# Cross-covariance attention with a mixture-of-depths step: the gate for held stores moved by one load, and the gate's vector spread by a matmul

## The chip, the cores and the metric

The kernel runs on one core of a Trainium2 chip. A core has five engines that run their own instruction streams: TensorE (PE; its weight loads are listed as PEld), VectorE (DVE), ScalarE (ACT), GpSimd (POOL) and SyncE (SP). Sixteen DMA engines move data between the memory (HBM) and the core's own memory (SBUF). The metric is the time of one execution on the device in microseconds (us), as the median of several runs. The profile is of one execution; its span, 264.0 us, is a little shorter than the time of that run, 265.82 us.

## What is computed

The reference, cut to what matters:

```python
# q, k, v: (4, 6208, 256) fp32; tau = 1; w_gate: (256,); w1: (256, 1024); w2: (1024, 256)
qn = q / (norm(q, axis=1) + 1e-6)              # norm of each channel over the 6208 rows
kn = k / (norm(k, axis=1) + 1e-6)
a  = softmax(kn.transpose(0, 2, 1) @ qn / tau) # 256 x 256 for each batch
x  = v @ a                                     # (4, 6208, 256)

scores = x @ w_gate                            # one number for each row
for b in range(4):
    top_idx = the 128 rows of batch b with the highest scores
    ye = relu(x[b, top_idx] @ w1) @ w2
    out[b, top_idx] = x[b, top_idx] + sigmoid(scores[b, top_idx])[:, None] * ye
# all other rows: out = x
```

For each batch all of q and k must be read before `a` is known, and all of v before the 128 rows can be chosen. q, k and v are 76 MB together, the output is 25 MB.

## The kernel before

The rows of a batch are cut into six chunks of 1024 rows (8 for each of the 128 partitions) and a rest of 64. q, k and v are read by GpSimd's queue, with a cast to bf16 on the way. The list of loads, `units`, has the order in which they are needed; a load is issued as soon as its pool has a free buffer (four pairs of q and k chunks, six v chunks).

```python
    QK_BUFS = 4
    V_BUFS = 6
    ...
    def emit_load(u):                       # q and k of a chunk, or v of a chunk
        ...
                    ins = nc.gpsimd.dma_start(out=t, in_=view(src, b, ci))
        ...
        load_inst[u] = ins

    pump(4)                                 # the first four units: four pairs of q and k
```

Next come the two weight matrices, on SyncE's queue, and constants. The vector `w_gate` is wanted in every partition, and the kernel before reads it 128 times:

```python
        for dst, src, inner in ((w1_sb, moe_w1, F), (w2_sb, moe_w2, D)):
            raw = st_pool.tile([P, RPP, C], F32, name="stage")...
            nc.sync.dma_start(out=raw, in_=src.rearrange("(k p) n -> p k n", p=P))
            nc.scalar.copy(dst, raw)
    ...
    ones_f = const.tile([P, P], F32)
    nc.vector.memset(ones_f, 1.0)
    ...
    wg_bcast = const.tile([P, C], F32)
    nc.sync.dma_start(out=wg_bcast, in_=moe_w_gate.partition_broadcast(P))

    wrow = const.tile([P, B, NCOL + 1], F32)       # and more small constants on VectorE
    ...
    pump()                                  # further loads, as buffers come free
```

The first pass over a batch multiplies chunks of q and k on TensorE. When the last row of a chunk has been used, its buffers are free:

```python
            for cc in range(2):
                nc.tensor.matmul(s_ps[:, cc, :], lhsT=ks[:, sl], rhs=qs, ...)
                nc.tensor.matmul(g_ps[:, cc, :], lhsT=qs[:, sl], rhs=qs[:, sl], ...)
                nc.tensor.matmul(g_ps[:, 2 + cc, :], lhsT=ks[:, sl], rhs=ks[:, sl], ...)
```

The softmax follows, whose last stage is the first reader of the vector:

```python
            nc.vector.tensor_tensor_reduce(out=awj, in0=a_sb[:, cc, :], in1=wg_bcast, ...,
                                           accum_out=aw[:, cc:cc + 1])
```

The second pass transposes v (`vt_ps`), forms the output rows (`o_ps`) and copies them to `stage`, 1 MB each, from which SyncE's queue stores them. The selection of the 128 rows is cut into small stages that are put between other work. The program's order is kept on every engine (`tc.manual_schedule()`): instructions run in the order in which the code emits them.

Some stores of the second and third batch are held back (`deferred`), so that they do not share the DMA engines with the loads that the end of the run waits for. The first of them waits for one of the last loads, and the others come after it on the same queue:

```python
    def flush_deferred(n=1000):

        while deferred and n > 0:
            st = emit_store(*deferred.pop(0))
            if not gate_done:
                gate_done.append(1)
                tc.add_manual_dep(
                    st.ins, load_inst[units[-3]].ins.name,
                    mybir.DependencyInfo(mybir.DependencyClass.Sync, mybir.DependencyReason.DATA),
                    reason="stores behind the last loads")
            n -= 1
```

The last units are the seven v loads of the last batch: `units[-1]` is the rest of 64 rows, `units[-2]` the sixth chunk, `units[-3]` the fifth, `units[-4]` the fourth.

Of the kernel before, what the change touches and what calls it, by code (L numbers as in the profile page):

```python
# [9 lines left out]
F32 = mybir.dt.float32  # L10
# [7 lines left out]
P = 128  # L18
# [8 lines left out]
def kernel(  # L27
# [12 lines left out]
    nc = tc.nc  # L40

    B, N, C = q.shape
# [23 lines left out]
    const = ctx.enter_context(tc.tile_pool(name="const", bufs=1))  # L66
# [15 lines left out]
    ps_m = ctx.enter_context(tc.tile_pool(name="ps_m", bufs=1, space=PS))  # L82
# [66 lines left out]
    units = []  # L149
# [6 lines left out]
    load_inst = {}  # L156
# [67 lines left out]
    ones_f = const.tile([P, P], F32)  # L224
# [15 lines left out]
    nc.gpsimd.iota(iota_col, pattern=[[0, 1]], base=0, channel_multiplier=1,  # L240
                   allow_small_or_imprecise_dtypes=True)
    wg_bcast = const.tile([P, C], F32)
    nc.sync.dma_start(out=wg_bcast, in_=moe_w_gate.partition_broadcast(P))


    wrow = const.tile([P, B, NCOL + 1], F32)
# [16 lines left out]
    rhs = const.tile([P, NCOL + 4], BF16)  # L263
# [270 lines left out]
    def emit_store(b, ci):  # L534
        st = stage_of.pop((b, ci))
        ins = nc.sync.dma_start(out=view(out, b, ci), in_=st if ci < NFULL else st[:REM, 0, :])
        stores.append((b, ins))
        for o, sca in scatters:
            if o != b:
                tc.declare_no_dep(ins.ins, sca.ins, reason="rows of different batches")  # L540
        return ins
# [215 lines left out]
# [4 lines that stand above are left out]
            if not gate_done:  # L761
                gate_done.append(1)
                tc.add_manual_dep(
                    st.ins, load_inst[units[-3]].ins.name,
                    mybir.DependencyInfo(mybir.DependencyClass.Sync, mybir.DependencyReason.DATA),
                    reason="stores behind the last loads")
            n -= 1
# [70 lines left out]
    keep_warm(8)  # L838
    advance(side)
    flush_deferred()  # L840
    while side2:
        advance(side2)
# [52 lines left out]
```

## Time and profile before

| what | value |
|---|---|
| time, median of 3 runs | 265.98 us (265.81 to 266.06) |
| span of the profiled execution | 264.0 us |
| PE busy | 201.2 us (76%) |
| DVE busy | 121.2 us (46%) |
| ACT busy | 81.5 us (31%) |
| POOL busy | 55.7 us (21%) |
| DMA, moved as counted at its writing side | 66.97 MB, mean 254 GB/s |
| HBM read and written | 79.04 MB and 25.95 MB |

The busy time is the union of an engine's instructions over the span. The page also cuts the span into 40 slices of 6.6 us and gives for each the busy share of every engine in tenths. A chain of waits is followed back from the last instruction: at each step it names what released it. Lines such as `L291` are lines of the kernel's source; `x24` is a count; in square brackets behind an instruction stands the idle time before it and what ended it. In tables by stretches the last three columns are TensorE's granted clock, the share of DMA engines that were busy, and GB/s.

### The profile page before, as it was taken

Reading aid. Unit: us, or ns where it says so; the run is one execution under the profiler, and the core shown is the slowest. Engines: PE = TensorE matmul, PEld = TensorE weight load, DVE = VectorE, ACT = ScalarE, POOL = GpSimd, SP = SyncE. Lnnn points to the kernel's source line nnn. Section 1 sums busy time; section 2 is a strip of 40 time slices with the busy share of each in tenths; the row PEclk is TensorE's granted clock in tenths of the full one; section 3 lists DMA queues with packets and bytes.
Section 4 is the critical chain, followed back from the end, with each engine's and each line's share of the span. In section 5 each row is a group of like instructions: output and inputs, shape, how many; then the busy total and the mean of one; then the engine's idle time right before and its main releaser. Section 6 shows DMA issues by size and latency. Waiting matters only on the chain.

```text
span 264.0 us, 6087 instructions
## 1 busy us (share of the span) xinstructions
PE 201.2 (76%) x2584; PEld 177.0 (67%) x2584; DVE 121.2 (46%) x464; ACT 81.5 (31%) x146; POOL 55.7 (21%) x104
## 2 busy tenths in 40 slices
PE   0194987899937677799986886899999899789700
PEld 0183876789926566589975775898999688578500
DVE  0200002614404366613436985674885827867400
ACT  3101100167720000117730100435102866795200
POOL 7113124121110023321300324320432003010110
PEclk9997699999998799799989999999999999999965
DMA  7999999999999999999999999999999999999950
GB/s 221 228 228 229 216 209 217 210 217 277 320 317 317 297 216 211 214 214 210 313 317 246 213 213 221 214 212 214 214 209 213 213 290 400 416 389 406 420 246 0
DMA packets 17642, 66.97 MB, mean 254 GB/s; under 512 B 2000, under 2 KB 4688, under 8 KB 14544
## 3 DMA queue, kind: packets, MB, share of 16 engines
q0 software_dynamic: 12384, 38.93, 73.8%
q1 hardware_dynamic: 5232, 27.66, 26.5%
q8 instruction: 20, 0.33, 0.4%
q14 instruction: 6, 0.05, 0.0%
HBM read 79.04 MB, written 25.95 MB: 398 GB/s over the span
## 4 chain that ended last, share of the span: by engine, by line
DMA 54%; PE 19%; issue 12%; DVE 8%; POOL 2%; ACT 1%; POOLq 1%; DVEq 0%; SPq 0%
DMA k_ch<-in_k_dram 22%; DMA q_ch<-in_q_dram 17%; DMA v_ch<-in_v_dram 12%; PE o_ps L477 5%; PE s_ps L291 4%; DMA out_dram<-stage 3%; PE g_ps L293 2%; PE vt_ps L403 2%; PE g_ps L295 2%; DVE cnt L588 1%; DVE cmp L584 1%; PE sc_ps L431 1%; DVE junk L310 1%; DVE stage L483 1%; PE g_ps L477 1%
## 5 line engine op out<-in xcount | busy, mean ns | idle before, releaser
L291 PE MATMUL s_ps<-q_ch,k_ch 128*128 128x256 bf16 x384 | 97.4, 293 | 30.1 <-DMA k_ch<-in_k_dram 29.5
L293 PE MATMUL g_ps<-q_ch 128*128 128x128 bf16 x384 | 89.0, 232 | 1.1 <-DVE nsq L310 1.0
L295 PE MATMUL g_ps<-k_ch 128*128 128x128 bf16 x384 | 88.9, 232 | 0.0
L291 PEld LDWEIGHTS <-k_ch 128*128 128x128 bf16 x384 | 40.3, 105 | 35.1 <-DMA k_ch<-in_k_dram 32.1
L295 PEld LDWEIGHTS <-k_ch 128*128 128x128 bf16 x384 | 40.2, 105 | 8.7 <-issue 1.6
L477 PE MATMUL o_ps<-a_sb,vt_sb 128*128 128x256 bf16 x298 | 43.9, 271 | 1.9 <-ACT vt_sb L410 1.3
L485 ACT COPY stage<-o_ps 128x512 f32<-128x512 f32 x68 | 38.3, 590 | 15.6 <-PE o_ps L477 15.6
L293 PEld LDWEIGHTS <-q_ch 128*128 128x128 bf16 x384 | 40.2, 105 | 1.2 <-issue 0.9
L412 DVE COPY vt_sb<-vt_ps 128x1024 bf16<-128x1024 bf16 (+1 forms) x33 | 20.8, 633 | 31.2 <-PE vt_ps L403 31.2
L477 PEld LDWEIGHTS <-vt_sb 128*128 128x128 bf16 (+1 forms) x376 | 29.4, 97 | 8.1 <-issue 4.4
L403 PE MATMUL vt_ps<-ident_b,v_ch 128*128 128x128 bf16 x336 | 24.6, 219 | 1.4 <-DMA v_ch<-in_v_dram 0.7
L431 PEld LDWEIGHTS <-vt_sb 128*128 128x128 bf16 (+1 forms) x376 | 23.8, 96 | 2.5 <-DVE sc L552 0.2
L174 POOL DMA_DIRECT2D q_ch<-in_q_dram x23 | 12.7, 553 | 59.9 <-PE g_ps L295 38.2
L403 PEld LDWEIGHTS <-v_ch 128*128 128x128 bf16 x384 | 22.2, 97 | 3.8 <-DMA v_ch<-in_v_dram 2.6
L306 ACT COPY s_sb<-s_ps 128x512 f32<-128x512 f32 x4 | 2.3, 586 | 71.3 <-PE s_ps L291 41.1
L431 PE MATMUL sc_ps<-aw_sb,vt_sb 128*128 128x2 bf16 (+1 forms) x376 | 24.2, 164 | 0.0
L310 DVE CUSTOM_DVE_ANT_0 junk<-g_ps,ident_f 128x128 f32<-128x128 f32 x16 | 4.6, 290 | 38.7 <-PE g_ps L295 38.3
L174 POOL DMA_DIRECT2D v_ch<-in_v_dram x24 | 12.8, 540 | 23.3 <-DMA k_ch<-in_k_dram 11.2
L174 POOL DMA_DIRECT2D k_ch<-in_k_dram x23 | 12.6, 546 | 21.8 <-PE o_ps L477 10.7
L588 DVE TENSOR_REDUCE cnt<-cmp 128x7 bf16<-128x343 bf16 x28 | 14.4, 513 | 1.0
L410 ACT COPY vt_sb<-vt_ps 128x1024 bf16<-128x1024 bf16 x11 | 10.6, 1011 | 12.8 <-PE vt_ps L403 12.7
L584 DVE SCALAR_TENSOR_TENSOR cmp<-u,delta,shares 128x343 bf16<-128x343 f32 x24 | 13.9, 578 | 0.9
(156 smaller groups left out, 213.0 us busy)
## 6 DMA issues: line engine op xcount, KB each, us to landing
out_dram<-stage SPq DMA_DIRECT2D x24, 1024.0 KB, 9.1
v_ch<-in_v_dram POOLq DMA_DIRECT2D x24, 512.0 KB, 14.8
q_ch<-in_q_dram POOLq DMA_DIRECT2D x23, 512.0 KB, 17.0
k_ch<-in_k_dram POOLq DMA_DIRECT2D x23, 512.0 KB, 17.4
stage<-in_moe_w_dram SPq DMA_DIRECT2D x2, 1024.0 KB, 14.6
q_ch<-in_q_dram POOLq DMA_DIRECT2D x2, 256.0 KB, 8.9
k_ch<-in_k_dram POOLq DMA_DIRECT2D x2, 256.0 KB, 9.7
out_dram<-stage_rem SPq DMA_DIRECT2D x4, 64.0 KB, 8.0
```

Of the source, the lines that this page charges most:

```text
L174: ins = nc.gpsimd.dma_start(out=t, in_=view(src, b, ci))
L291: nc.tensor.matmul(s_ps[:, cc, :], lhsT=ks[:, sl], rhs=qs, start=first and cc == 0, stop=last and cc == 1)
L293: nc.tensor.matmul(g_ps[:, cc, :], lhsT=qs[:, sl], rhs=qs[:, sl], start=first and cc == 0, stop=False)
L295: nc.tensor.matmul(g_ps[:, 2 + cc, :], lhsT=ks[:, sl], rhs=ks[:, sl], start=False, stop=last and cc == 1)
L403: nc.tensor.transpose(vt_ps[:, cc, j, :parts], in_=vt[:parts, s0 + j, cc * P:(cc + 1) * P], identity=ident_b[:parts, :parts])
L410: nc.scalar.copy(vt_sb[:, :, :n, :parts], vt_ps[:, :, :n, :parts])
L412: nc.vector.tensor_copy(vt_sb[:, :, :n, :parts], vt_ps[:, :, :n, :parts])
L431: nc.tensor.matmul(sc_ps[:parts, col, :], lhsT=vt_sb[:, cc, j, :parts], rhs=aw_sb[:, cc, :], start=cc == 0 and col in (0, NCOL - 1), stop= ...
L477: nc.tensor.matmul(o_ps[:parts, pj, :], lhsT=vt_sb[:, cc, j, :parts], rhs=a_sb[:, cc, :], start=pj == 0 and cc == 0, stop=pj == m - 1 and ...
L485: nc.scalar.copy(st[:parts, s0 + pair * 2:s0 + pair * 2 + m, :], o_ps[:parts, :m, :])
L584: nc.vector.scalar_tensor_tensor(out=cmp, in0=wide, scalar=delta, in1=thr, op0=ALU.subtract, op1=ALU.is_ge)
L588: nc.vector.tensor_reduce(out=cnt, in_=cmp, axis=AX.X, op=ALU.add)
```

## The change

There are two edits. The first reads the gate's vector once, into one partition, and spreads it over all 128 by a matmul with a row of ones, whose result VectorE copies from PSUM (TensorE's output memory) to `wg_bcast`; this is meant to take 127 of 128 reads off the DMA engines. The second lets the held stores begin when the fourth of the last six v chunks has landed, instead of the fifth; this is meant to leave the DMA engines no pause between the last loads and the first held stores.

```diff
@@ -240,7 +240,11 @@
     nc.gpsimd.iota(iota_col, pattern=[[0, 1]], base=0, channel_multiplier=1,
                    allow_small_or_imprecise_dtypes=True)
     wg_bcast = const.tile([P, C], F32)
-    nc.sync.dma_start(out=wg_bcast, in_=moe_w_gate.partition_broadcast(P))
+    wg_row = const.tile([1, C], F32)
+    nc.sync.dma_start(out=wg_row, in_=moe_w_gate.partition_broadcast(1))
+    wg_ps = ps_m.tile([P, 512], F32, name="m_ps")
+    nc.tensor.matmul(wg_ps[:, 0:C], lhsT=ones_f[0:1, :], rhs=wg_row, start=True, stop=True)
+    nc.vector.tensor_copy(wg_bcast, wg_ps[:, 0:C])
 
 
     wrow = const.tile([P, B, NCOL + 1], F32)
@@ -761,7 +765,7 @@
             if not gate_done:
                 gate_done.append(1)
                 tc.add_manual_dep(
-                    st.ins, load_inst[units[-3]].ins.name,
+                    st.ins, load_inst[units[-4]].ins.name,
                     mybir.DependencyInfo(mybir.DependencyClass.Sync, mybir.DependencyReason.DATA),
                     reason="stores behind the last loads")
             n -= 1
```

## The prediction

> **What bounds the kernel now.** I read the page's slices first, then its chain, then the start and the tail in the timelines.
>
> ```profile
> DMA  7999999999999999999999999999999999999950
> GB/s 221 228 228 229 216 209 217 210 217 277 320 317 317 297 216 211 214 214 210 313 317 246 213 213 221 214 212 214 214 209 213 213 290 400 416 389 406 420 246 0
> ...
> DMA 54%; PE 19%; issue 12%; DVE 8%; POOL 2%; ACT 1%; POOLq 1%; DVEq 0%; SPq 0%
> ```
>
> The sixteen DMA engines are busy in every slice from the second to the thirty-seventh (the loads show about 215 GB/s because they are counted after the cast from fp32 to bf16). So the rule for this kernel is: time in which the DMA engines stand idle is added to the end one for one, and work on another engine costs nothing unless it makes them stand idle. The two edits touch two places where they could.
>
> The start, from the timeline of GpSimd (which issues the loads) and of the others:
>
> ```profile
> 5.22 0.61 POOL L174 DMA_DIRECT2D k_ch<-in_k_dram  x1
> ...
> 18.25 0.57 POOL L174 DMA_DIRECT2D q_ch<-in_q_dram  x1 [10.40 <-PE g_ps L295]
> ```
>
> ```profile
> 12.04 0.39 PE L291 MATMUL s_ps<-q_ch,k_ch 128*128 128x256 bf16 x1 [12.04 <-DMA k_ch<-in_k_dram]
> ```
>
> ```profile
> 25.48 1.90 ACT L215 CAST w_sb<-stage 128x2048 bf16<-128x2048 f32 x1 [17.71 <-DMA stage<-in_moe_w_dram]
> ```
>
> Four pairs of q and k are issued at once (the last at 5.22); the fifth waits for a buffer, that is for TensorE to finish the first pair. TensorE starts at 12.04 and the fifth pair is issued at 18.25, 6.2 us later. The fourth pair lands at about 28.9 on most engines, so today the refill comes 10 us early. The last line is the second weight matrix, which lands only at 25.45 although it is issued at 1.3.
>
> ```profile
> wg_bcast<-in_moe_w_gate_dram SPq DMA_DIRECT2D x1, 128.0 KB, 25.9
> ```
>
> The gate's vector is third on the same queue and lands 25.9 us after its issue at 1.81, at 27.7. Nobody waits for it: its first reader runs at 50.4.
>
> The tail, from the chain in order of time, the waits of the store queue and a table by stretches:
>
> ```profile
> 200.02 15.77 DMA v_ch<-in_v_dram
> ...
> 215.84 0.62 PE s_ps L403 x8
> ```
>
> ```profile
> SPq L536 <- DMA v_ch<-in_v_dram: 77.0, 1, 77.0
> ```
>
> ```profile
> 212.00:213.00 1.00, 1.00 (x11) 0.90 (x10) 0.00 (x0) 0.75 (x2) 0.00 (x0) 1.00 0.74 133
> 213.00:214.00 1.00, 0.77 (x12) 0.49 (x11) 0.00 (x0) 0.58 (x1) 0.00 (x0) 1.00 0.61 123
> 214.00:215.00 1.00, 1.00 (x34) 1.00 (x32) 0.69 (x1) 0.37 (x1) 0.00 (x0) 1.00 1.00 328
> ```
>
> ```profile
> 213.50 3.11 SPq L536 DMA_DIRECT2D out_dram<-stage  x4
> ```
>
> ```profile
> 222.17 7.33 SPq L536 DMA_DIRECT2D out_dram<-stage  x4
> ```
>
> Four held stores wait for the load units[-3] (the fifth of the last six v chunks) and leave at 213.50. Between 212 and 214 the DMA share (the last but one column) falls to 0.74 and 0.61: some 0.65 us of all engines is lost there, which is what the edit aims at. The last v chunk releases TensorE at 215.84 and starts the last selection. The fifth store needs output that comes after it in TensorE's order, and goes out at 222.17.
>
> **What the Trainium skill says.** (1) "DMA: Bandwidth & Descriptors", section "Queues, rings and completion order": each DMA engine takes turns between the queues that have work and consumes one queue's descriptors in order. The trace agrees: the second weight matrix, 64 packets of 1 KB on each engine, needs from 5.8 to 23.6 beside the loads, 0.28 us a packet, the time of the 4 KB load packet in between; alone the same packet takes 0.06. (2) The same page, "Why a DMA increments its semaphore by 16 and not by 1": a transfer counts as landed when every engine it uses has finished; so a short transfer lands as late as its place in the queues. The trace agrees: 13 engines end the second matrix by 23.84, the last at 25.45, and ScalarE starts at 25.48. (3) "Perfetto Trace Analysis", section "Sequencer Loop": an engine's sequencer takes the next instruction, which then waits for its semaphores. I read it as order: nothing behind it starts. The trace fits; TensorE's first instruction holds all others until 12.04. (4) "TensorE: Matmul & The Clock Gate", section "What's actually happening": after idleness the clock is half and recovers after some 3.4 us of work. Here the matmuls are 0.42 us from 12.04 to 16.7 and 0.27 after it, so the half clock lasted 4.7.
>
> **Part one: the vector through a matmul.** Removed: 128 packets of 1 KB, 8 an engine. Beside them the loads moved at some 45 packets a us and without at 53, for 2.2 us: 17 packets, 0.3 us of DMA saved. Added: one 1 KB row, one fp32 matmul, one PSUM copy on VectorE. The order of the built kernel settles the rest: the matmul is the *first* instruction of TensorE, ahead of the first q and k, and it waits for the row. The row is still third on its queue, behind both weight matrices. So TensorE starts not at 12.04 but when the row lands.
>
> When: most engines are done with the weights at 23.8 and the row needs one turn more: 24.1. In the trace before, one engine was 1.6 us late, just when an instruction fetch of 16 KB ran; with TensorE standing still that fetch should come later. I take 24.4, range 23.8 to 25.8.
>
> From there to the fifth pair: it was 6.2 us. The matmul with fp32 (two passes at L342 fill 0.70 us warm) is about 1.3 at half clock, an estimate; it uses up half-clock time, in which a row of the chunk takes 0.85 against 0.45, so the net addition is 0.6 to 0.8. 24.4 + 7.0 = 31.4, and with some 1.2 us from issue to first packet (an estimate: the last scatter, into idle engines, took 1.5) the loads resume at 32.6. The engines run dry at 28.5 to 28.9. Against the old flow that is a loss of 32.6 - 28.9 = 3.7 us, with the 0.3 saved already in it. TensorE then takes 3.6 us a chunk and the DMA 4.8, so the stream does not break again, and nothing later in the run gives the loss back because the DMA has no idle time there. VectorE's setup of 2 us also moves behind the copy, to about 26 to 29; its first use is after 40, so it costs nothing.
>
> **Part two: the gate one load sooner.** units[-4] has landed at 210.0 (on the slowest engine), so the four stores leave 3.5 us sooner and their first packets come at 210.9 instead of 214.3. That fills the 0.65 us hole. But at 210.9 eight engines have 3.8 us of v still to load. With stores in the other queue each load packet waits a turn. GpSimd's issues, each held until an old load has landed, show the price while stores ran earlier:
>
> ```profile
> 73.72 0.52 POOL L177 DMA_DIRECT2D q_rem<-in_q_dram  x1 [4.18 <-DMA q_ch<-in_q_dram]
> 78.72 0.52 POOL L177 DMA_DIRECT2D k_rem<-in_k_dram  x1 [4.47 <-DMA k_ch<-in_k_dram]
> ```
>
> 5.0 us apart, against 2.4 without stores (50.49 to 52.96). So 3.8 us become 7.7, and v lands at 218.5 to 219.8 instead of 215.8: the selection, and every output behind it, comes up to 4.0 us later. The fifth store goes out at 226.2 and its packets start at 227.0; the four early stores (10 us) are finished by 223 to 225. Before, they were finished at 225.1 and the fifth store had been waiting 2.1 us. So the hole of 0.65 us at 213 is traded for one of about 2 us at 225, into which a gather and a scatter of 0.5 us fit. All later stores have 2.6 to 3.9 us of slack (landing less issue less 3.3 us), so that the shift doesn't grow: about +1.0, range -0.7 to +2.
>
> **Sum.** 265.98 + 3.7 + 1.0 = 270.7; I say 270.8.
>
> **Rivals.** (a) *The row comes early*, because it is tiny and might not queue behind the weights: then TensorE starts near 12 and only the fp32 matmul remains, hidden by the 10 us that the refill is early. For it: one packet is little. Against it: the old vector's packets came strictly after the second matrix. It would give 265.5 to 267. (b) *The gate is a pure gain*: the hole is filled and the late v is hidden by the backlog of stores, whose last takes 8.1 us to land. Then part two is -0.7 and the total 269.0. The slack of 2.6 us at the fifth store speaks for half of this. (c) *The start costs more*: the late engine is late again and the clock stays at half longer, 25.8 + 7.6 + 1.5 = 34.9: a loss of 6.0, in all 273.0. (d) *The late start is caught up*, since TensorE has slack: against it, that the DMA and not TensorE is the bound.
>
> **Range and chances.** (b) and (c) give the range, 268.6 to 273.2. The limit of 2% is 271.3, just above my centre, so slower by over 2% has 0.42 and within 2% 0.55; for faster, (a) and (b) would both have to hold and bring more than 2%, which the holes seen do not contain: 0.03.
>
> **What would show it.** TensorE's first instruction, the matmul on wg_row, should start near 24.4 after a wait for that load; the fifth q issue near 31.4 instead of 18.25; a slice of the DMA row below 9 near 29 to 33; the first stores at 210 + 3.7 = 213.7, the last v some 8 us after them, and the wait of the fifth store longer than the backlog. A TensorE start near 12 proves part one wrong; a last v less than 6 us after the gate proves the sharing wrong.

## The result, and the profile after

| | before | changed |
|---|---|---|
| time, median | 265.89 us (265.66 to 266.06) | 273.98 us (273.38 to 274.53) |
| ratio | | 1.0304, 95% interval 1.0274 to 1.0334 |
| span of the profiled execution | 264.0 us | 272.7 us |

The change costs 8.1 us. It was predicted at 270.8, at most 273.2, with a chance of 0.42 for slower by over 2%: the direction was right, the size was outside the range.

The page's slices and chain of the changed kernel:

```profile
DMA  7999299999999999999999999999999997799960
GB/s 221 226 234 221 44 211 211 216 213 204 309 316 315 316 253 211 214 214 211 285 312 270 213 212 222 213 211 214 214 210 213 221 391 275 326 383 371 421 264 0
...
DMA 45%; PE 34%; DVE 9%; issue 5%; ACT 1%; POOL 1%; POOLq 0%; SPq 0%; DVEq 0%
```

Two holes are new in the DMA row: the fifth slice has fallen from 9 to 2, and the 34th and 35th from 9 to 7. TensorE's share of the chain has grown from 19% to 34%.

The start. First ScalarE's cast of the second weight matrix and TensorE's first instruction, then GpSimd's issue of the fifth pair, all from the timeline; last the table by stretches (its last but one column is the DMA share):

```profile
24.61 1.90 ACT L215 CAST w_sb<-stage 128x2048 bf16<-128x2048 f32 x1 [16.87 <-DMA stage<-in_moe_w_dram]
...
24.65 1.19 PE L246 MATMUL m_ps<-wg_row,ones_f 1*128 1x256 f32 x2 [24.65 <-DMA wg_row<-in_moe_w_gate_dram]
```

```profile
31.38 0.57 POOL L174 DMA_DIRECT2D q_ch<-in_q_dram  x1 [23.54 <-PE g_ps L299]
```

```profile
28.00:30.00 2.00, 2.00 (x21) 1.77 (x20) 0.00 (x0) 0.00 (x0) 0.00 (x0) 1.00 0.01 0
30.00:32.00 2.00, 2.00 (x30) 1.90 (x28) 0.00 (x0) 0.00 (x0) 0.62 (x2) 1.00 0.00 0
32.00:34.00 2.00, 2.00 (x30) 1.90 (x28) 0.00 (x0) 0.00 (x0) 0.48 (x1) 1.00 0.54 72
```

The one-row load lands with the second weight matrix. TensorE, which used to start at 12.04, waits for it until 24.65; the fifth pair is issued at 31.38 instead of 18.25, and from 28 to 32 the DMA engines do next to nothing. In the trace, q of the fifth pair lands on the median engine at 36.25 instead of 31.37, so 4.9 us are gone.

The tail, first from the chain in order of time, then the stores' issues, then the stretches (TensorE's granted clock and the DMA share are the third and second column from the right):

```profile
206.43 18.03 DMA v_rem<-in_v_dram
...
224.51 0.29 PE vt_ps L407 x2
```

```profile
215.86 2.88 SPq L540 DMA_DIRECT2D out_dram<-stage  x4
```

```profile
231.97 0.33 SPq L540 DMA_DIRECT2D out_dram<-stage  x1
```

```profile
225.00:230.00 5.00, 5.00 (x72) 4.33 (x71) 1.80 (x12) 1.51 (x3) 1.75 (x2) 0.50 0.81 329
230.00:235.00 5.00, 5.00 (x31) 3.71 (x29) 2.84 (x10) 3.42 (x7) 0.27 (x1) 0.59 0.63 236
```

The four held stores leave at 215.86. The rest of v lands at 224.46, 8.6 us after them; before, the same rest landed at 216.0, 2.5 us after the gate. The hole before the first held stores is gone, but the share is 0.81 and 0.63 between 225 and 235, the ten us after the landing of v. The ten us after it in the kernel before:

```profile
215.00:220.00 5.00, 4.89 (x116) 4.35 (x113) 2.22 (x11) 2.63 (x4) 0.64 (x1) 1.00 1.01 416
220.00:225.00 5.00, 4.42 (x39) 3.71 (x40) 3.77 (x13) 3.76 (x8) 1.38 (x2) 1.00 1.00 375
```

The share was full there. And there is something that was not there before: TensorE's clock is at half, from 223.8 to 234.05. TensorE's work ahead of this, first before, then in the changed kernel:

```profile
214.43 1.34 PE L431 MATMUL sc_ps<-aw_sb,vt_sb 128*128 128x2 bf16 x48
215.84 0.62 PE L403 MATMUL s_ps<-ident_b,v_ch 128*128 128x128 bf16 x8
```

```profile
220.06 1.34 PE L435 MATMUL sc_ps<-aw_sb,vt_sb 128*128 128x2 bf16 x48
223.06 0.62 PE L407 MATMUL s_ps<-ident_b,v_ch 128*128 128x128 bf16 x8 [1.66 <-DMA v_ch<-in_v_dram]
```

The same 48 matmuls of two columns are followed by a wait of 0.07 us before and of 1.66 us now. From the landing of v to the issue of the sixth store it takes 10.7 us (235.13 - 224.46), before 8.4 (224.40 - 216.0).

### The profile page after: what moved, and what is told of

Its sections match the earlier page's. It is cut to its first block, busy times and chain, and to the rows that moved or that the text cites. A ratio compares the mean times of both kernels' runs of the same rounds, so it can differ in the third digit from the quotient of the medians.

```text
span 272.7 us, 6092 instructions
## 1 busy us (share of the span) xinstructions
PE 202.5 (74%) x2586; PEld 177.6 (65%) x2586; DVE 121.8 (45%) x465; ACT 82.1 (30%) x146; POOL 55.5 (20%) x104
## 4 chain that ended last, share of the span: by engine, by line
DMA 45%; PE 34%; DVE 9%; issue 5%; ACT 1%; POOL 1%; POOLq 0%; SPq 0%; DVEq 0%
DMA k_ch<-in_k_dram 17%; DMA wg_row<-in_moe_w_gate_dram 8%; PE s_ps L295 8%; PE o_ps L481 8%; DMA v_rem<-in_v_dram 7%; DMA v_ch<-in_v_dram 6%; DMA q_ch<-in_q_dram 5%; PE g_ps L299 4%; PE g_ps L297 4%; PE vt_ps L407 3%; DMA out_dram<-stage 2%; DVE cmp L588 2%; DVE cnt L592 2%; PE sc_ps L435 1%; PE g_ps L481 1%
## 5 line engine op out<-in xcount | busy, mean ns | idle before, releaser
L295 PE MATMUL s_ps<-q_ch,k_ch 128*128 128x256 bf16 x384 | 93.9, 286 | 13.0 <-DMA k_ch<-in_k_dram 11.7
L297 PE MATMUL g_ps<-q_ch 128*128 128x128 bf16 x384 | 87.3, 227 | 1.8 <-DVE nsq L314 1.8
L299 PE MATMUL g_ps<-k_ch 128*128 128x128 bf16 x384 | 87.4, 227 | 0.0
L295 PEld LDWEIGHTS <-k_ch 128*128 128x128 bf16 x384 | 39.4, 103 | 18.0 <-DMA k_ch<-in_k_dram 14.4
L481 PE MATMUL o_ps<-a_sb,vt_sb 128*128 128x256 bf16 x298 | 45.8, 280 | 1.9 <-ACT vt_sb L414 1.3
L299 PEld LDWEIGHTS <-k_ch 128*128 128x128 bf16 x384 | 39.4, 102 | 8.5 <-issue 2.3
L297 PEld LDWEIGHTS <-q_ch 128*128 128x128 bf16 x384 | 39.3, 102 | 1.5 <-issue 1.2
L481 PEld LDWEIGHTS <-vt_sb 128*128 128x128 bf16 (+1 forms) x376 | 31.0, 101 | 8.9 <-issue 3.8
L435 PEld LDWEIGHTS <-vt_sb 128*128 128x128 bf16 (+1 forms) x376 | 24.0, 98 | 2.6 <-DVE sc L556 0.2
L246 PE MATMUL m_ps<-wg_row,ones_f 1*128 1x256 f32 x2 | 1.2, 694 | 24.6 <-DMA wg_row<-in_moe_w_gate_dram 24.6
```

Of the source, the lines that this page charges most:

```text
L295: nc.tensor.matmul(s_ps[:, cc, :], lhsT=ks[:, sl], rhs=qs, start=first and cc == 0, stop=last and cc == 1)
L435: nc.tensor.matmul(sc_ps[:parts, col, :], lhsT=vt_sb[:, cc, j, :parts], rhs=aw_sb[:, cc, :], start=cc == 0 and col in (0, NCOL - 1), stop= ...
L481: nc.tensor.matmul(o_ps[:parts, pj, :], lhsT=vt_sb[:, cc, j, :parts], rhs=a_sb[:, cc, :], start=pj == 0 and cc == 0, stop=pj == m - 1 and ...
```

## The experiments

The theory after this profile (A): two losses that add up, the idle start and the tail. The rivals are named with each run.

**The two parts alone.** e1 has only the second edit, e2 only the first.

```diff
# e1: the kernel before, with
-                    st.ins, load_inst[units[-3]].ins.name,
+                    st.ins, load_inst[units[-4]].ins.name,
# e2: the changed kernel, with units[-3] again
```

> Only the gate is moved to the fourth of the last six v chunks; the vector is loaded 128 times as before. Theory A (two separate losses that add up: 4.9 us from TensorE's late start, about 3.3 us from held stores that slow the last v loads): about 269.2 us, the last v load lands some 8 us after the gate opens, later than before by about 3 us, and the fifth held store goes out about 5 us later than before. Rival B (the gate fills the pause between loads and stores, and the whole loss comes from the start): about 265.2 us. Rival C (the gate costs only because the late start made the last loads late): about 266.

> Only the vector is loaded as one row and spread by the matmul at the head of TensorE's order; the gate stays where it was before. Theory A: about 270.8 us, TensorE starts near 24.6, the fifth pair of loads is issued near 31.4 and the DMA engines stand idle for some 4.6 us from 28.4 on; nothing of it is regained later. Rival B: about 274, the whole loss.

Measured: e1 268.06 us (266.97 to 269.27), ratio 1.0076 (1.0051 to 1.0102), 2.0 us. e2 271.48 us, ratio 1.0192 (1.0155 to 1.0229), 5.4 us by the medians and 5.1 by the ratio. Together 7.4 of the 8.1. Rival B falls on both: neither part is the whole loss and the gate is no gain. e1 also shows that the gate costs without any late start, against rival C. But e1 is 1.1 us below what was expected, and its runs lie 2.3 us apart, which the sharing of transfers does not explain. In its trace the last v lands 8.5 us after the gate, as expected (218.64 against 210.17), which is 2.6 us later than before and not 3; the fifth store goes out 3.0 us later (225.13) and not 5. e2 is 0.7 us above its 270.8.

**What in the first part costs.** Three ways to change the wait at the head of TensorE's order. e3 leaves the load where it is and moves matmul and copy behind the first batch's first pass; e4 leaves the matmul at the head and moves the load ahead of the weights; e9 keeps the old 128 reads and only adds the matmul at the head, so that the wait is for a load that lands still later. All three have the old gate.

```diff
# e3: in softmax_stages(b), instead of among the constants
+        if b == 0:
+            wg_ps = ps_m.tile([P, 512], F32, name="m_ps")
+            nc.tensor.matmul(wg_ps[:, 0:C], lhsT=ones_f[0:1, :], rhs=wg_row, start=True, stop=True)
+            nc.vector.tensor_copy(wg_bcast, wg_ps[:, 0:C])
# e4: ahead of the weights
+    wg_row = const.tile([1, C], F32)
+    nc.sync.dma_start(out=wg_row, in_=moe_w_gate.partition_broadcast(1))
     w1_sb = const.tile([P, C // P, F], BF16)
# e9: the kernel before, with
     nc.sync.dma_start(out=wg_bcast, in_=moe_w_gate.partition_broadcast(P))
+    wg_ps = ps_m.tile([P, 512], F32, name="m_ps")
+    nc.tensor.matmul(wg_ps[:, 0:C], lhsT=ones_f[0:1, :], rhs=wg_bcast[0:1, :], start=True, stop=True)
+    wg_copy = const.tile([P, C], F32)
+    nc.vector.tensor_copy(wg_copy, wg_ps[:, 0:C])
```

> One row and a matmul as in the changed kernel, but matmul and copy stand in the program after the first batch's first pass, ahead of its softmax; the gate stays as before. Theory A (the cost of part one is the wait at the head of TensorE's order, not the matmul, the copy or the one-row load): 265.6 us, TensorE starts near 12 and the DMA engines are never idle at the start. Rival D (the matmul or VectorE's copy themselves cost, or a one-row load disturbs the queue): above 267.

> One row, the matmul at the head of TensorE's order as in the changed kernel, but the row's load is issued ahead of the two weight matrices; the gate stays as before. Theory A (the row lands late because it stands behind the weights in one queue): the row lands within about 4 us of the start, TensorE starts with q and k near 12 as before, time about 265.6 us. Rival E (a one-row load or the matmul's place in the order is slow in itself): TensorE starts well after 12, time above 267.

> The kernel before with its 128 reads of the vector, and in addition the same matmul at the head of TensorE's order, reading one row of the loaded vector (its result is only copied to a tile that nobody reads). Theory A (each us by which the first matmul comes later, beyond the slack of the first loads, is a us of idle DMA engines): the vector lands at 27.7 and not 24.6, TensorE starts there, so the time is 3.0 us above the 271.4 of e2: 274.4. Rival D (the cost belongs to the one-row load): 266 to 267.

Measured: e3 265.34 us, ratio 0.9974 (0.9959 to 0.9990); e4 265.70 us, ratio 0.9993 (0.9980 to 1.0006); e9 275.33 us, ratio 1.0356 (1.0337 to 1.0376). TensorE's first instruction in e3, e4, e2 and e9, from their timelines; for e2 and e9 also the issue of the fifth pair:

```profile
12.08 0.40 PE L292 MATMUL s_ps<-q_ch,k_ch 128*128 128x256 bf16 x1 [12.08 <-DMA k_ch<-in_k_dram]
```

```profile
6.87 1.22 PE L246 MATMUL m_ps<-wg_row,ones_f 1*128 1x256 f32 x2 [6.87 <-DVE ones_f L227]
11.96 0.39 PE L295 MATMUL s_ps<-q_ch,k_ch 128*128 128x256 bf16 x1 [3.88 <-DMA k_ch<-in_k_dram]
```

```profile
24.07 1.19 PE L246 MATMUL m_ps<-wg_row,ones_f 1*128 1x256 f32 x2 [24.07 <-DMA wg_row<-in_moe_w_gate_dram]
...
31.60 0.57 POOL L174 DMA_DIRECT2D q_ch<-in_q_dram  x1 [23.76 <-PE g_ps L299]
```

```profile
28.12 1.19 PE L245 MATMUL m_ps<-wg_bcast,ones_f 1*128 1x256 f32 x2 [28.12 <-DMA wg_bcast<-in_moe_w_gate_dram]
...
35.40 0.57 POOL L174 DMA_DIRECT2D q_ch<-in_q_dram  x1 [27.55 <-PE g_ps L299]
```

In e4 the same load and the same matmul, in the same place, cost nothing, because nobody waits for the load: the matmul waits for the row of ones, and q and k come as before. In e3 the late row (it lands at 24.87) costs nothing, because its reader comes late, at 43.65. In e9 there is no one-row load at all. TensorE starts 4.05 us later than in e2, the fifth pair is issued 3.80 us later, and the time is 3.85 us longer (4.15 when each is set against the kernel before of its own comparison). In the traces q of the fifth pair lands 5.0 us later than before in e2 (36.40 against 31.37) and 9.0 us in e9 (40.34); the times are 5.1 to 5.4 and 9.5 us longer: about a us for each us. (e2's trace is of its slowest run, 273.44 us; only its start is used. e9 is 0.9 us above its 274.4.) So rivals D and E fall, and the cost is shown to be the wait at the head of an in-order queue for a load behind 2 MB of others.

**How the gate's place acts.** Two more places for it, on the kernel before.

```diff
# e5
+                    st.ins, load_inst[units[-5]].ins.name,
# e6
+                    st.ins, load_inst[units[-2]].ins.name,
```

> The kernel before with the gate two loads sooner (units[-5], the third of the last six v chunks). Theory A (held stores double the time of every load that is still to come, and the last loads start the selection and the stores behind it): the stores go out near 207.5, 6.3 us of loads are left on the slower DMA engines and take 12.6, the last v lands near 221.5, the pause ahead of the fifth store grows to some 3 to 4 us: 269.5 us (268.5 to 271.5). Rival B (sooner is better or free): 266 or less.

> The kernel before with the gate one load later (units[-2], the sixth v chunk). Theory A: the pause between loads and stores grows by 2.3 us (stores start near 216.7 and not 214.3), the last v lands no later than before, and the stores up to the end follow without a pause: 268.0 us. So units[-3] is the best of the four gates. Rival C (the pause is hidden, because the stores wait for TensorE's output anyway): 266.

Measured: e5 270.53 us, ratio 1.0178 (1.0148 to 1.0208), 1.0 us above the expected centre and inside its range; e6 268.63 us, ratio 1.0111 (1.0074 to 1.0148), 0.6 us above the expected 268.0. Rivals B and C fall. With e1 the row is 270.5, 268.1, 266.0, 268.6 for units[-5], [-4], [-3], [-2]: the gate of before stood at the best of the four. Where the time goes is to be seen in the DMA share: a stretch of the kernel before, the same of e6, then three of e5:

```profile
214.00:217.00 3.00, 2.94 (x78) 2.70 (x75) 1.20 (x2) 1.07 (x2) 0.00 (x0) 1.00 1.01 387
```

```profile
214.00:217.00 3.00, 2.82 (x77) 2.63 (x74) 1.06 (x2) 1.01 (x1) 0.00 (x0) 1.00 0.25 65
```

```profile
217.00:222.00 5.00, 2.30 (x29) 1.95 (x26) 0.69 (x1) 0.22 (x2) 0.00 (x0) 0.50 1.03 412
222.00:224.00 2.00, 2.00 (x22) 1.48 (x21) 0.27 (x2) 1.60 (x3) 0.00 (x0) 0.57 0.62 258
224.00:226.00 2.00, 1.81 (x55) 1.63 (x51) 1.34 (x9) 0.50 (x1) 0.80 (x1) 1.00 0.18 70
```

Too late a gate leaves the hole ahead of the held stores (e6); too early a gate moves it behind them, since the last v lands at 221.56 (expected: near 221.5) and the fifth store goes out at 228.0 instead of 222.2. In e5, too, TensorE is at half clock, for 6.8 us from 216.9 on, after a wait of 1.7 us for v and through one of 2.7.

**The half clock.** The last open point was the spread of e1 and the part of the changed kernel's tail that the transfers don't explain. e7 is e1, e8 the changed kernel, e11 the kernel before, each with 28 matmuls of 128x128 whose results nobody reads, put ahead of the transposes of the last v chunk. They come from a helper that the kernel already has (`keep_warm`) and calls at two later places.

```diff
-    plan += T[8:10] + S[:6] + T[10:] + rest[:1] + [("side",)] + S[6:]
+    plan += T[8:10] + S[:6] + [("warm", L, 28)] + T[10:] + rest[:1] + [("side",)] + S[6:]
```

> As e1 (only the gate moved, to units[-4]), with 28 added 128x128 matmuls whose results nobody reads, in the time in which TensorE waits for the last v chunk. Theory A2 (the part of the gate's cost that the prediction lacks, and the spread of e1 between 267.0 and 269.3, is TensorE at half clock after that longer wait): TensorE's granted clock stays at 1.0 from the gate to the end of the tail, median 267.0 us, spread under 1 us. Rival: the spread comes from a late DMA engine; then the median stays at 268.1.

> The changed kernel, with the same 28 matmuls. Theory A2: the half clock between 224 and 234 goes away, and with it some 1.5 to 2 us: 272.2 us. Rival: 274.0, as the changed kernel.

> The kernel before, its gate unchanged (units[-3]), with the same 28 matmuls ahead of the last v chunk. It has no half clock in the tail to lose, so theory A2 (the matmuls help e7 and e8 only through the clock) expects no gain: the 1.6 us of added TensorE work come out of the slack of the fifth store, 266.0 to 266.6 us. Rival F (the added matmuls help in themselves, for instance by the place where they put the following work): 2 us less than before, about 264.

Measured: e7 266.04 us (265.57 to 266.79), ratio 1.0005 (0.9994 to 1.0017); e8 271.35 us, ratio 1.0212 (1.0179 to 1.0246); e11 266.15 us, ratio 1.0021 (1.0005 to 1.0038). Stretches behind the gate of e1, then the same of e7, then those of e8 that answer to the changed kernel's:

```profile
215.00:220.00 5.00, 3.55 (x54) 2.99 (x52) 0.91 (x2) 1.51 (x2) 0.00 (x0) 0.73 1.01 411
220.00:225.00 5.00, 4.81 (x82) 4.21 (x81) 2.65 (x15) 2.31 (x6) 2.02 (x2) 0.93 0.79 303
225.00:230.00 5.00, 4.07 (x37) 3.21 (x36) 4.33 (x15) 4.33 (x10) 0.00 (x0) 1.00 0.92 374
```

```profile
215.00:220.00 5.00, 4.43 (x84) 3.95 (x81) 0.92 (x2) 1.85 (x3) 0.00 (x0) 1.00 1.02 413
220.00:225.00 5.00, 4.70 (x83) 4.12 (x81) 3.48 (x16) 2.65 (x6) 2.02 (x2) 1.00 0.85 323
225.00:230.00 5.00, 4.10 (x37) 3.23 (x37) 4.33 (x16) 4.33 (x10) 0.00 (x0) 1.00 1.02 414
```

```profile
225.00:230.00 5.00, 4.52 (x76) 3.92 (x73) 3.48 (x16) 2.65 (x6) 2.02 (x2) 1.00 0.85 329
230.00:235.00 5.00, 4.28 (x39) 3.34 (x37) 4.43 (x17) 4.34 (x9) 0.00 (x0) 1.00 1.03 416
```

The clock stays at 1.00, and the whole cost of the gate is gone: from 2.0 us to nothing in e7, and the changed kernel falls by 2.6 us (2.4 by the ratios), to the 271.5 of e2. Without the half clock, the hole that is left (0.85 in five us, some 0.8 us) is about as large as the one that was filled. That is more than theory A2 expected, which gave the transfers one us of their own. The spread falls as well, from 2.3 us in e1 to 1.2 in e7 (expected: under 1). And within e1 the four slowest runs have a mean granted clock of 0.933, the four fastest of 0.944; e1's trace is of its fastest run. e11 rules out that the matmuls help in themselves: where the clock isn't lost they bring nothing and cost some 0.2%.

**A middle way for the gate.** e10 is e3 with only the first held store let go after units[-4] and the others after units[-3]; e3 was run again beside it.

```diff
-            if not gate_done:
+            if len(gate_done) < 2:
                 gate_done.append(1)
...
-                    st.ins, load_inst[units[-3]].ins.name,
+                    st.ins, load_inst[units[-4 if len(gate_done) == 1 else -3]].ins.name,
```

> As e3 (one row, matmul ahead of the first softmax), with only the first held store let go after units[-4] and the others after units[-3]. Theory A: the first store's 2.5 us fill the pause before 214, but delay the last v by up to 2.5 us, which the slack of the fifth store (2.1 to 2.6 us) just about covers: 264.9 us, and not above 265.8. Rival: the delay of the last v costs as much as the pause brought: 265.3 to 266.

> e3 again, on the same chip as e10, for the comparison of the two: 265.3 us.

Measured: e10 268.32 us, ratio 1.0074 (1.0048 to 1.0100); e3 again 265.41 us, ratio 0.9988 (0.9978 to 0.9999). e10 is a miss for the theory as I had used it: the last v landed 9.3 us after the first gate (220.73 against 211.42), where e3 has 6.1 us between the same two loads (215.77 against 209.66). That is a delay of 3.2 us and more than the store's 2.5, since the second store joined at 215.29, before v was in. Its trace (of its slowest run) has TensorE at half clock for 3.4 us, too, around the end of a wait of 1.78 us for v. Whether it would gain with the added matmuls was not tried. e3 stays the best version: 0.4 to 0.7 us faster than the kernel before, an advantage that just clears its intervals.

## Why the prediction was wrong, step by step

Both mechanisms, the wait at the head of TensorE's order and the sharing of the DMA engines with the held stores, were right; the sizes were not. Two steps failed: the restart of the loads after the fifth issue, which made the start 3.7 us instead of some 5, and "so that the shift doesn't grow: about +1.0" in the tail, which left out that TensorE loses its clock behind the longer wait, 2.6 us. A third error went the other way: the transfers of the tail cost nothing instead of 1.0.

- **The bound** ("time in which the DMA engines stand idle is added to the end one for one"): right at the start, where it was tried: 5.0 us of delay are 5.1 to 5.4 at the end of e2, 9.0 are 9.5 in e9.
- **The order of the built kernel** (the matmul first, waiting for a row behind the weights): right, with its numbers: 24.4 said, 24.65 measured; the fifth issue at 31.4 said, 31.38 measured. The 1.19 us of the fp32 matmul was put at 1.3. That the issue fits to 0.02 us is luck: e2 starts 0.6 us sooner and issues at 31.60, because the half clock lasts 6.3 us there and not 4.6 (by the durations of the first matmuls, 0.42 us each and then 0.27; the clock column shows 1.00 there, since its records begin with the change to full).
- **"With some 1.2 us from issue to first packet ... the loads resume at 32.6"**: too short. The earliest packets came at 32.7, but by 33.28 only eight had begun for sixteen engines, the first four took 1.1 to 1.2 us each instead of 0.32, and the load was complete on the median engine 4.9 us after its issue; the prediction's terms (1.2, and 2.45 for a 512 KB load in the full stream) make 3.65. That is the 1.2 us by which the start was under-rated: 4.9 and not 3.7.
- **Sharing with held stores**: the doubling was right, its extent not. The last v 8 us after the gate was said, 8.6 measured (8.5 in e1). In e1 the loads took 5.0 us on the median engine from the first store packet on, where the kernel before needs 2.6 from that time. But this packet came at 212.1, 1.9 us after the issue, and not at 210.9, so v was 2.6 us late and not up to 4.0.
- **The trade of one hole for another, "+1.0"**: the transfers alone cost 0.0 (e7), within the stated -0.7 to +2. With v only 2.6 us late the fifth store goes out at 224.27 in e7 and not at 226.2, and the hole behind the four stores is 0.8 us and not about 2.
- **The missing term.** The Trainium skill's "TensorE: Matmul & The Clock Gate", section "What's actually happening", has TensorE at half clock after at least one idle window of about 3.4 us, and at full clock after about as much sustained work. The prediction used this for the start only; the step "so that the shift doesn't grow" took TensorE in the tail at full speed, although it had just given it a longer wait. The page's figures would not have given the loss either: here waits of 1.45 us (e1) and 1.66 us (the changed kernel) behind the two-column matmuls were enough, and the half clock lasted 3.4 us in the profiled run of e1 but 10.2 in that of the changed kernel, with TensorE shown busy. It lies on the chain that feeds the stores. Its price is the difference with and without the added matmuls: 268.06 - 266.04 = 2.0 in e1, 273.98 - 271.35 = 2.6 in the changed kernel. Why it lasted three times as long there stays open.
- **The sum**: 265.9 + 5.4 + 0.0 + 2.6 = 273.9, measured 273.98, where 3.7 + 1.0 had been said. This checks the parts only in part, since the 2.6 is taken from the changed kernel itself. The range failed because its upper end joined a bad start with the gate's planned cost and left the clock out.
- **Rivals**: (a) fell with the row at 24.5; (b) was half right, for a TensorE that is kept busy; (c) named the start as costlier, though in the changed kernel's trace not for its reasons: the row came at 24.5 and the half clock lasted 4.6 us, as before (4.7); e2 and e9 do show a longer one (6.3 and 5.7); (d) fell, nothing was caught up.

## What to carry to other kernels

A constant that is built on TensorE stands in TensorE's queue: put its first instruction behind work that doesn't need it, or its load ahead of the large ones, and look at the order of the built kernel, not at the size of the load. Before a gate on stores is opened sooner, count what the loads behind it still have to do, double it (2.6 us became 5.0 here), and see who waits for the last of them. And where a change lengthens a wait of TensorE, look at the granted clock after the wait as well; a few matmuls without a reader can be cheaper than its loss, as e7 and e8 show.

## What the runs showed of the hardware

A load of 1 KB took 22.7 us, from 1.81 to 24.5, with nothing slow about it but its place behind two others; issued first, in e4, it took 1.25 us, from 0.81 to 2.06.

The first load into idle DMA engines took 4.9 us from issue to landing on the median engine (36.25 - 31.38); its twins in the full stream of the kernel before land 2.4 us after one another (31.37, 33.81, 36.24).

TensorE can lose its clock while it counts as busy. In the changed kernel it did 48 matmuls of two columns in 1.34 us and then waited 1.66 us for v; some 0.8 us into the next work the clock was at half and stayed there for 10.2 us, through stretches that the table shows as fully busy. In the kernel before, with the same 48 matmuls and 0.07 us of waiting, it stayed at full. Whether the two-column matmuls count as work for the clock was not tried; 28 matmuls of 128 columns behind them, 1.72 us, were enough to keep it in e7 and e8.
